# A second, tabulated order for the first work list of a three-stage kernel that plans its own instruction order

## The chip, the cores and the metric

The kernel runs on one core of one Trainium2 chip. The metric is the device time of one execution in microseconds (us); the median over the runs of a kernel is quoted. The core has five engines with instruction streams of their own: TensorE (PE; its weight loads are shown apart as PEld), VectorE (DVE), ScalarE (ACT), GpSimd (POOL) and SyncE (SP), which issues nearly all DMAs here. An instruction waits on semaphores for what it needs, and on one engine the instructions run in the order in which the program wrote them.

## The reference, cut to what matters

Three stages follow one another; the second takes the output of the first, the third that of the second.

```python
def attn(q, k, v):                  # 2 batches x 8 heads, 768 positions, 64 wide
    scores = q @ k.T / 8            # kept: window of 128 positions, and the first 4 (sinks)
    a = exp(scores - max); a /= sum(a) + 1e-09
    return a @ v                    # -> x, 2 x 768 x 512

def moe(x, w_gate, wq, wk, wv, wo): # 4 experts, every one over all tokens, causal
    logits = x @ w_gate; top 2 per token, w = softmax over the two
    for e in range(4):
        a = softmax(causal(x@wq[e] @ (x@wk[e]).T / 8))
        out += w[:, e] * (a @ (x@wv[e])) @ wo[e]

def moe2(x, w_gate, w_local, w1, w2):   # 8 experts of 512 x 1024 x 512, one per token
    fresh = argmax(x @ w_gate); p = softmax(x @ w_gate)
    e[s] = fresh[s] if s == 0 or sigmoid(x[s] @ w_local) < 0.5 else e[s-1]
    out[s] = p[s, e[s]] * relu(x[s] @ w1[e[s]]) @ w2[e[s]]
```

## The kernel before, in words

**The work.** Queries go in tiles of 128. A unit of attention work is a handful of score matrices: TensorE multiplies kT by qT into a PSUM bank (L699), VectorE adds the mask and takes the row maximum in one custom instruction (L713; its `nm` row is the maximum), ScalarE exponentiates (L723), TensorE transposes the result (L827), ScalarE copies the transposed block to float16 as the high half (L830), VectorE subtracts to get the low half (L834), and TensorE multiplies both halves by v (L842 to L844). In the second stage most of these halves are made before the transposition instead, by ScalarE (L782) and GpSimd (L787), and v is multiplied at L798 to L800. kT and qT come from transposes (L424) that ScalarE copies out of PSUM (L430). v of the first batch is scaled and split by ScalarE (L649) and VectorE (L653), later ones by GpSimd (L660, L663, L669); L609 takes the maxima of v for that scale, L532 joins them into `amax`, and L536 moves that across partitions. The sinks of one batch are gathered into `vbd` by GpSimd (L633 to L636). The first stage's result is scaled by L962 and L966 (the sums behind it by L339), the second's by L1098. Weights are split into a high and a low part by ScalarE (L478, later L1511 and L1513) and GpSimd or VectorE (L480, L1521). L1005 makes the low half of the second stage's v, L1025 to L1038 are the gate of the four experts, some dozen VectorE instructions on 128x8 numbers. The routing of the third stage (`route`) is a chain of small instructions: VectorE makes `r_ms` (L1296 to L1306), TensorE turns it (L1323), VectorE scans (L1327, L1329), TensorE turns back (L1335), VectorE makes the one-hot rows (L1337), TensorE counts with them (L1345, L1346), and VectorE turns counts into slots (L1350 to L1361) and these into permutations (L1369; GpSimd L1371). After that the lists of tokens are made, GpSimd writes the expert numbers `eui` (L1920), and SyncE loads the weights of the third stage's units by these numbers.

**The order.** None of this is written in the order in which it runs. Each piece is a `Task` with an engine, a planned duration, its dependences, the buffers that it takes (`acq`) and gives back (`rel`) and a priority, added to an `Order` object. `Order.run` is a greedy planner: it keeps a planned clock for each engine, takes the piece that can start first (ties by priority), books its planned duration, and emits its instructions at once. Durations come from formulas such as `d_v` (VectorE) and `d_a` (ScalarE), and latencies between engines from `LAT`; nothing in them depends on what another engine does at the time. `order.run()` of the first list covers the first two stages, the routing and the lists, some 250 us of the run; later calls plan the units of the third stage.

**Spins.** While the buffer "warm" is held (up to about 30 us, and again from about 205 us on), the planner puts idle matmuls of 128x512 (`spin`, L410) into the gaps that it foresees on TensorE: `int(gap / 0.22 * fill)` of them where a gap is over 0.3 us, with `fill` 0.5 in the first stretch and 1.0 in the second. They write to a bank that nobody reads, and TensorE executes them like any other matmul, in order.

Of the kernel before, what the change touches and what calls it, by code (L numbers as in the profile page):

```python
# [63 lines left out]
WT = (0, 3)  # L64
PC = 4
PSZ = 32
QU = 2
QN = 4
CLD = 0.4


class Task:
    __slots__ = ("eng", "dur", "fn", "deps", "acq", "rel", "prio", "end", "name", "rows", "fills", "lat", "slack", "hold")

    def __init__(self, eng, dur, fn, deps, acq, rel, prio, rows=False):
        self.eng, self.dur, self.fn, self.prio, self.rows = eng, dur, fn, prio, rows
        self.deps = [d for d in deps if d is not None]
        self.acq, self.rel = list(acq), list(rel)
        self.end = None
        self.fills = False  # L80
        self.lat = None
        self.slack = 0.0
        self.hold = 0.0


class Order:
# [7 lines left out]
    def __init__(self, bufs, named):  # L94
# [6 lines left out]
        self.fill = FILL  # L101
        self.rows = False

    def add(self, eng, dur, fn, deps=(), acq=(), rel=(), prio=0, rows=False):
# [21 lines left out]
    def run(self):  # L126
        todo = sorted(self.tasks, key=lambda t: t.prio)
        while todo:
            best = {}
            for part in (todo[:400], todo[400:]):  # L130
                for t in part:
                    e = self.ready(t)
# [18 lines left out]
            if t.eng == "PE" and "warm" in self.held and gap > 0.3:  # L151
                for _ in range(int(gap / 0.22 * self.fill)):
                    self.spin()
            t.end = e + t.dur
            self.free[t.eng] = t.end
            if t.eng == "PE":
                self.rows = t.rows
            for tag, name in t.acq:
                ring = self.slots[tag]
                k = min((i for i, x in enumerate(ring) if x is not None), key=lambda i: ring[i])  # L160
                self.held[name] = (tag, k)
                self.named[name] = self.bufs[tag][k]
                ring[k] = None
            for name in t.rel:
                tag, k = self.held.pop(name)
                self.slots[tag][k] = t.end + (t.lat or self.LAT[t.eng])
            todo.remove(t)
            t.fn()
        self.tasks = []

    def state(self):
# [40 lines left out]
def fused_kernel(  # L212
# [96 lines left out]
    K = {}  # L309
# [1225 lines left out]
    def turnover():  # L1535
        blocks_.close()
        own = ctx.enter_context(tc.tile_pool(name="own", bufs=1, side="right", reuse_waits="tile"))
        for tag, n, tiles in (("xg", 1, [([128, DM], F32)]), ("hs", 2, [([128, 512], F32)]),
# [6 lines left out]
                        + [K["S1", b, i, u] for b in range(B) for i in range(NT) for u in range(UN1)]  # L1545
                        + [K.get(("skm", b, i)) for b in range(B) for i in range(NT)], prio=at2(B - 1, 0))
    last_sc = []

# [186 lines left out]
    for t in order.tasks[n_:]:  # L1735
        t.fills = t.eng in ("PE", "ACT", "DVE")
    order.run()
    front.close()
# [257 lines left out]
```

## Time and profile before

| | |
|---|---|
| time, median of 3 runs | 409.21 us (409.04 to 410.77) |
| the profiled execution's own time | 411.15 us |
| its span, from first to last instruction | 409.4 us |
| TensorE clock granted over it, mean | 0.998 |
| VectorE busy, with 1005 rows | 325.1 us |
| ScalarE busy, with 758 rows | 317.9 us |
| GpSimd busy, with 288 rows | 166.8 us |
| DMA, all queues | 58.75 MB in 101501 packets |

The span is 1.75 us shorter than the execution's own time, which also holds what lies around the instructions, and the profiled execution is 1.94 us above the median of the timed runs. "Busy" counts an instruction from its start to its end, so a matmul that has been issued and is still flowing through the array counts as busy too. A timeline row joins consecutive instructions of one line and shape (its xcount) and gives their start, the time they cover, and in brackets how long the engine stood idle before and which instruction released it. A tile's name in the trace has no buffer number.

### The profile page before, as it was taken

How to read it: one execution, taken by the hardware profiler on the slowest of the kernel's cores; microseconds unless marked ns; L12 is line 12 of the kernel's file. 1: busy time of each engine (PE TensorE's matmuls, PEld its weight loads, DVE VectorE, ACT ScalarE, POOL GpSimd, SP SyncE). 2: the span in 40 equal slices, each digit the busy share in tenths (PEclk: the TensorE clock that was granted, in tenths of full speed). 3: DMA queues.
4: the chain of work that ended last, by engine and by line, in shares of the span. 5: the costliest groups of instructions: out<-in, count | busy, mean ns of one | idle time of the engine just before them, and what ended most of it. 6: DMA issues, size and time to landing. Idle time of an engine off the chain costs nothing. (4 is left out here: it accounts for less than half of the span.)

```text
span 409.4 us, 10290 instructions
## 1 busy us (share of the span) xinstructions
PE 394.5 (96%) x3339; PEld 312.8 (76%) x3339; DVE 325.1 (79%) x1005; ACT 317.9 (78%) x758; POOL 166.8 (41%) x288
## 2 busy tenths in 40 slices
PE   8899999999999999999998999999999999999993
PEld 4569988969879877988876777746666888888883
DVE  2998599497889688779899899866576788899680
ACT  4799799669999789965698428867577898888770
POOL 7378985267976637710627015020101310110100
PEclk9999999999999999999999999999999999999999
DMA  7998298824987743820561112958879951110001
GB/s 152 187 209 194 67 175 141 160 72 79 183 153 141 130 95 66 143 61 20 201 214 53 38 67 85 344 201 313 303 236 391 388 195 40 51 53 27 33 22 57
DMA packets 101501, 58.75 MB, mean 143 GB/s; under 512 B 83903, under 2 KB 85439, under 8 KB 101440
## 3 DMA queue, kind: packets, MB, share of 16 engines
q1 hardware_dynamic: 99280, 51.21, 49.3%
q0 software_dynamic: 2160, 6.82, 4.8%
q8 instruction: 28, 0.46, 0.4%
q14 instruction: 33, 0.27, 0.2%
HBM read 82.39 MB, written 6.55 MB: 217 GB/s over the span
## 5 line engine op out<-in xcount | busy, mean ns | idle before, releaser
L723 ACT ACTIVATE P<-P,nm 128x260 f32<-128x260 f32 (+3 forms) x100 | 53.1, 535 | 12.0 <-DVE nm L713 11.6
L713 DVE CUSTOM_DVE_ANT_0 P<-bank,masks 128x260 f32<-128x260 f32 (+3 forms) x84 | 36.5, 463 | 8.1 <-PE bank L699 8.0
L787 POOL TENSOR_TENSOR raw<-PX,raw 128x512 f16<-128x512 f32 (+2 forms) x34 | 35.6, 1051 | 16.5 <-ACT raw L782 14.4
L834 DVE TENSOR_TENSOR pT<-bank,pT 128x512 f16<-128x512 f32 (+1 forms) x50 | 30.7, 630 | 8.4 <-ACT pT L830 8.3
L699 PE MATMUL bank<-kT,qT 64*128 64x260 f32 (+1 forms) x192 | 31.8, 405 | 2.3 <-POOL kT L597 1.1
L723 ACT ACTIVATE PX<-PX,nm 128x260 f32<-128x260 f32 (+4 forms) x60 | 30.6, 513 | 2.5 <-DVE nm L713 2.4
L1521 DVE TENSOR_TENSOR wo<-raw,wo 128x1024 fp32r<-128x1024 f32 x23 | 27.8, 1220 | 3.2 <-ACT wo L1513 2.6
L424 PE MATMUL bank<-ident,raw 128*128 128x128 f32 x168 | 28.3, 292 | 1.2 <-DVE r L339 0.4
L830 ACT ACTIVATE pT<-bank 128x512 f16<-128x512 f32 (+1 forms) x50 | 26.0, 551 | 3.9 <-PE bank L827 3.6
L324 PE MATMUL bank<-xT,wqk_h 128*128 128x256 f32 x96 | 28.5, 297 | 0.0
L325 PE MATMUL bank<-xT,wqk_h 128*128 128x256 f32 x96 | 26.7, 278 | 0.0
L326 PE MATMUL bank<-xT,wqk_l 128*128 128x256 f32 x96 | 26.7, 278 | 0.0
L699 PEld LDWEIGHTS bank<-kT,qT 64*128 64x128 f32 x192 | 19.1, 191 | 9.9 <-issue 2.1
L827 PE MATMUL bank<-ident,P 128*128 128x128 f32 x180 | 26.5, 277 | 0.2 <-DVE nm L713 0.2
L1521 DVE TENSOR_TENSOR w<-raw,w 128x1024 fp32r<-128x1024 f32 x19 | 22.9, 1222 | 4.5 <-ACT w L1513 4.4
L1513 ACT ACTIVATE wo<-raw 128x1024 fp32r<-128x1024 f32 x23 | 24.0, 1057 | 3.0 <-PE bank L326 2.7
L424 PEld LDWEIGHTS bank<-ident,raw 128*128 128x128 f32 x168 | 20.5, 164 | 7.4 <-DVE nm L713 2.0
L713 DVE CUSTOM_DVE_ANT_0 PX<-bank,masks 128x260 f32<-128x260 f32 (+4 forms) x60 | 23.4, 426 | 2.4 <-PE bank L699 2.3
L699 PE MATMUL bank<-k,q 64*128 64x256 f32 (+3 forms) x128 | 24.4, 466 | 0.1
L1617 ACT ACTIVATE hs<-bank 128x512 f32<-128x512 f32 x24 | 14.4, 599 | 10.7 <-PE bank L326 10.7
L1521 DVE TENSOR_TENSOR wqk_l<-raw,wqk_h 128x1024 fp32r<-128x1024 f32 x17 | 20.8, 1226 | 2.3 <-ACT wqk_h L1513 2.2
L1689 POOL DMA_INDIRECT out_dram<-masks,six x6 | 6.9, 1147 | 38.2 <-ACT masks L1682 33.0
(504 smaller groups left out, 1467.9 us busy)
## 6 DMA issues: line engine op xcount, KB each, us to landing
raw<-in_moe_w_dram SPq DMA_DIRECT2D x96, 512.0 KB
qw<-in_moe_w_dram SPq DMA_DIRECT2D x32, 512.0 KB
raw<-in_v_dram SPq DMA_DIRECT2D x12, 256.0 KB
x2d<-x SPq DMA_DIRECT2D x12, 256.0 KB
raw<-in_q_dram SPq DMA_DIRECT2D x11, 256.0 KB
raw<-in_k_dram SPq DMA_DIRECT2D x11, 256.0 KB
pT<-raw SPq DMA_TRANSPOSE x46
raw<-in_moe_wv_dram SPq DMA_DIRECT2D x1, 512.0 KB
```

What stands on the lines that cost most here:

```text
L324: nc.tensor.matmul(o, l[0], r[0], start=start, stop=False)
L325: nc.tensor.matmul(o, l[0], r[1], start=False, stop=False)
L326: nc.tensor.matmul(o, l[1], r[0], start=False, stop=stop)
L424: nc.tensor.transpose(p[:, j * 128:(j + 1) * 128], src(j), ident)
L699: nc.tensor.matmul(o, l, r, start=True, stop=True)
L713: nc.vector.tensor_tensor_reduce(p, s, sg["mask"], 0.0 if dead and st == 1 else -scale, gr["nm"] if si else 3.0e38, op0=OP.add, op1=OP.min ...
L723: nc.scalar.activation(p, p, AF.Exp, bias=gr["nm"], scale=-1.0, accum_out=sg["sum"]())
L787: nc.gpsimd.tensor_sub(shaped(pl[:, s_], dims), p_, shaped(ph[:, s_], dims))
L827: nc.tensor.transpose(R[tk][:, j * 128:(j + 1) * 128], R[gr["P"]][:, c:c + 128], ident)
L830: nc.scalar.activation(R[sk_][:, :n * 128], R[tk][:, :n * 128], AF.Copy)
L834: nc.vector.tensor_sub(pl[:, :n * 128], R[tk][:, :n * 128], ph[:, :n * 128])
L1521: eng.tensor_sub(wl[:, :, s_], R["raw", u, c, hf][:, :, s_], f32(wh)[:, :, s_])
```

## The change

The greedy planner still runs over the first list, but while it runs it emits nothing: it assigns the buffers, notes for each piece what it took and gave, and collects the pieces in a list (`seq`). Then `flush` goes through a table of numbers, `TURNS`, and emits the collected pieces in that order. The list is cut in two at the piece `turnover` (`stays = True`), where the space of the first stage's blocks goes to buffers of the third stage; the table's first string has 1432 numbers for what comes before it, the second 407 for what comes after. Buffers, dependences, instructions and their sizes stay as they were. Only the number of spins is worked out anew, from the planned gaps of the new order by the same formula, with turn-round times `IN` and `OUT`. The table was computed beforehand; by the words that came with the change, with a plan that counts GpSimd's hold on VectorE's operations. Later lists are planned as before.

```diff
+IN, OUT = 0.095, 0.19
...
+TURNS = (
+    "0 2-16 19 21 17 24 20 22 18 23 28 25-27 29 1 30-32 37 33-36 38 41-43 48 40 55 47 39 45-46 50 52-53 44 49 54 "
...
+    "1-5 0 6 10 7 17 8 11 22 13 12 9 15 19 14 26 18 16 20 24-25 32 21 23 36 27 29 28 30-31 37 39 43 33 35 40-42 34 "
...
+def unpacked(texts):
+    runs = [[[int(x) for x in r.split("-")] for r in t.split()] for t in texts]
+    return [[n for r in rs for n in range(r[0], r[-1] + 1)] for rs in runs]
...
@@ Order.run @@
             if t.eng == "PE" and "warm" in self.held and gap > 0.3:
-                for _ in range(int(gap / 0.22 * self.fill)):
-                    self.spin()
+                if self.seq is None:
+                    for _ in range(int(gap / 0.22 * self.fill)):
+                        self.spin()
...
+                t.spins = self.fill if "warm" in self.held else False
...
-            t.fn()
+            if self.seq is None or t.stays:
+                self.flush()
+                self.go(t)
+                t.fn()
...
+            else:
+                self.seq.append(t)
...
+    def flush(self):
...
+        turns = self.turns.pop(0)
...
+        for n in turns:
+            t = seq[n]
...
+            if t.eng == "PE":
+                if t.spins and self.hot and gap > 0.3:
+                    for _ in range(int(gap / 0.22 * t.spins)):
+                        self.spin()
...
+            end[t] = free[t.eng] = e + t.dur
...
+            if t.eng != "J":
+                t.fn()
...
+    K["turnover"].stays = True
...
+    order.seq, order.turns = [], unpacked(TURNS)
     order.run()
```

Comparing the instruction streams of the two kernels: TensorE's real work stands in the same order, and 11 of the 37 spins are gone, six in the first stretch and five in the second; a few others stand elsewhere. SyncE's 823 rows, all the DMA issues on its queue among them, are the same in the same order. VectorE has the same 1089 rows (read accumulators counted apart), of which about 323 stand elsewhere, ScalarE the same 719 with about 151 elsewhere, GpSimd the same 343 with about 43 elsewhere. Behind the first list nothing differs. The lines of the change lie 139 or so below those of before: L713 is L852 there, L834 is L973, L609 is L748, L653 is L792, L339 is L478, L430 is L569, L478 is L617, L723 is L862, L830 is L969, L1306 is L1445, L1361 is L1500, L1369 is L1508, L1562 is L1702.

**First place: VectorE at about 14 to 17 us,** the first blocks of queries. P4 and P0 are masked scores, v0 and v1 the split v, vmax the maxima of the next v, r1 the reciprocal sums. Before:

```order
L653 SCALAR_TENSOR_TENSOR v0_1_100<-raw2_0_85,s_se0_461,v0_0_99 128x512
L609 TENSOR_REDUCE vmax0_236<-raw3_0_86 128x1
L653 SCALAR_TENSOR_TENSOR v1_1_102<-raw2_0_85,s_se0_461,v1_0_101 128x512
L339 TENSOR_REDUCE r1_0_0_237<-sums1_149 128x8
L609 TENSOR_REDUCE vmax0_236<-raw3_0_86 128x1
L962 RECIPROCAL r1_0_0_237<-r1_0_0_237 128x8
L713 ISA P4_0_111,nm_522<-bank7_82,masks_158 128x260
L713 ISA nm_522 128x1
L713 ISA P4_0_111,nm_525<-bank1_76,masks_158 128x260
```

And in the change:

```order
L792 SCALAR_TENSOR_TENSOR v0_1_100<-raw2_0_85,s_se0_469,v0_0_99 128x512
L748 TENSOR_REDUCE vmax0_236<-raw3_0_86 128x1
L852 ISA P4_0_111,nm_504<-bank7_82,masks_158 128x260
L852 ISA nm_504 128x1
L852 ISA P0_0_107,nm_506<-bank5_80,masks_158 128x260
L852 ISA nm_506 128x1
L852 ISA P4_0_111,nm_508<-bank1_76,masks_158 128x260
L852 ISA nm_508 128x1
L478 TENSOR_REDUCE r1_0_0_237<-sums1_149 128x8
```

The masks of P4 and P0 now stand right behind the first vmax. The second split of v (v1) has gone 19 rows down, behind the low half of pT0, and the second vmax stands behind four masks.

**Second place: ScalarE at about 25 to 31 us.** wvg_h and wqk_h are the high parts of the second stage's weights, kT the transposed keys of the third block. Before:

```order
L478 ACTIVATE wvg_h_208<-raw0_0_83 128x256 x4
L830 ACTIVATE pT2_0_114<-bank2_77 128x512
L830 ACTIVATE pT3_0_115<-bank4_79 128x512
L723 ACTIVATE P3_0_110,sums1_149<-P3_0_110,nm_650 128x260
L723 ACTIVATE P3_0_110,sums1_149<-P3_0_110,nm_657 128x260
L478 ACTIVATE wqk_h_206<-raw1_0_84 128x256 x4
L430 ACTIVATE kT_212<-bank3_78 128x4x128
```

And in the change:

```order
L969 ACTIVATE pT2_0_114<-bank2_77 128x512
L617 ACTIVATE wvg_h_208<-raw0_0_83 128x256
L969 ACTIVATE pT3_0_115<-bank4_79 128x512
L862 ACTIVATE P4_0_111,sums1_149<-P4_0_111,nm_668 128x260
L862 ACTIVATE P3_0_110,sums1_149<-P3_0_110,nm_647 128x260
L569 ACTIVATE kT_212<-bank3_78 128x4x128
L617 ACTIVATE wqk_h_206<-raw1_0_84 128x256
L617 ACTIVATE wvg_h_208<-raw0_0_83 128x256
L862 ACTIVATE P4_0_111,sums1_149<-P4_0_111,nm_671 128x260
```

Of the eight weight pieces that stood ahead of kT, seven stand behind it, spread singly over the next rows; one exponential of P4 has come ahead of it.

**Third place: VectorE at about 219 to 223 us,** the last tiles, where r_ms opens the last pass of the routing chain; slot and v2h belong to an earlier pass, ux is the input of a third-stage unit. Before:

```order
L834 TENSOR_TENSOR pT1_0_113<-bank2_77,pT1_0_113 128x512
L1358 TENSOR_SCALAR rk_319<-rk_319 128x2
L1304 TENSOR_REDUCE mxs_321<-LG_233 128x1
L1296 SCALAR_TENSOR_TENSOR r_fr10_334<-LG_233,s0_291 128x1
L1361 TENSOR_SCALAR slot_320<-rk_319 128x2
L1305 SCALAR_TENSOR_TENSOR r_sc10_332<-LG_233,mxs_321,rev8_286 128x8
L1369 TENSOR_SCALAR v2h0_215<-iot_287,slot_320,tok_294 128x128 x2
L1306 ISA r_sc10_332,r_ms10_333<-r_sc10_332,r_fr10_334 128x8
L1306 ISA r_ms10_333 128x1
L834 TENSOR_TENSOR pT3_0_115<-bank5_80,pT3_0_115 128x512
L1562 TENSOR_TENSOR ux0_1_3422<-bank4_79,ux0_0_3421 128x512
```

And in the change:

```order
L1435 SCALAR_TENSOR_TENSOR r_fr10_334<-LG_233,s0_291 128x1
L1444 SCALAR_TENSOR_TENSOR r_sc10_332<-LG_233,mxs_321,rev8_286 128x8
L1496 TENSOR_REDUCE rk_319<-r_sc8_330 128x2
L1702 TENSOR_TENSOR ux0_1_3416<-bank4_79,ux0_0_3415 128x512
L1445 ISA r_sc10_332,r_ms10_333<-r_sc10_332,r_fr10_334 128x8
L1445 ISA r_ms10_333 128x1
L1497 TENSOR_SCALAR rk_319<-rk_319 128x2
L973 TENSOR_TENSOR pT3_0_115<-bank5_80,pT3_0_115 128x512
L1500 TENSOR_SCALAR slot_320<-rk_319 128x2
L1466 TENSOR_SCALAR raw7_0_90<-bank2_77 1x128
L1508 TENSOR_SCALAR v2h0_215<-iot_287,slot_320,tok_294 128x128
```

The pieces of the earlier pass (rk, slot, v2h) that stood ahead of r_ms stand behind it, and the 128x512 piece of ux has come ahead of it.

## Rows read from the trace of the kernel before

**Rows 1.** The page's first part: busy time, share of the span and instructions.

```profile
PE 394.5 (96%) x3339; PEld 312.8 (76%) x3339; DVE 325.1 (79%) x1005; ACT 317.9 (78%) x758; POOL 166.8 (41%) x288
```

**Rows 2.** Busy time by stretch: length; PE, PEld, DVE, ACT, POOL; clock; DMA share; GB/s.

```profile
0.00:215.00 215.00, 208.87 (x2260) 173.60 (x2260) 173.35 (x754) 179.57 (x571) 129.59 (x241) 1.00 0.65 135
215.00:226.00 11.00, 9.89 (x115) 7.28 (x114) 10.93 (x44) 9.20 (x21) 7.89 (x18) 1.00 0.13 49
...
272.00:397.00 125.00, 125.00 (x645) 93.94 (x638) 98.05 (x96) 98.67 (x125) 16.20 (x16) 1.00 0.50 177
...
14.00:22.00 8.00, 7.31 (x74) 5.22 (x75) 8.00 (x25) 5.85 (x18) 0.00 (x0) 1.00 0.90 148
26.00:31.00 5.00, 4.67 (x48) 2.86 (x48) 4.86 (x22) 5.00 (x17) 4.70 (x7) 1.00 1.12 213
```

**Rows 3.** PE's waits, 0 to 215 us: line, releaser, total us, times, longest.

```profile
PE bank L699 <- POOL kT L597: 1.1, 1, 1.1
PE bank L699 <- DVE nm L713: 0.7, 1, 0.7
PE bank L424 <- DVE r L339: 0.4, 1, 0.4
```

**Rows 4.** Timeline at the first list's end, then the chain that ended last (start, us).

```profile
246.03 0.30 POOL L1920 CAST eui<-euf 36x3 int32<-36x3 f32 x1 [7.09 <-DVE euf L1919]
...
256.21 8.45 DMA qw<-in_moe_w_dram
```

**Rows 5.** The spins: their line over the run (ns min/median/max), and the first four.

```profile
L410 PE MATMUL bank<-v2h x37: 377/379/634, 1.3 to 243.6; 128*128 128x512 f16 x37
...
1.25 1.89 PE L410 MATMUL bank<-v2h 128*128 128x512 f16 x4 [1.25 <-DVE v2h L414]
```

**Rows 6.** Timeline, 14 to 18 us: DVE and PE (start, us, engine, line).

```profile
15.05 0.74 DVE L653 SCALAR_TENSOR_TENSOR v<-raw,s_se,v 128x512 f16<-128x512 f32 x1
15.79 0.67 DVE L609 TENSOR_REDUCE vmax<-raw 128x1 f32<-128x512 f32 x1
16.49 0.38 DVE L713 CUSTOM_DVE_ANT_0 P<-bank,masks 128x260 f32<-128x260 f32 x1
16.93 0.44 PE L827 MATMUL bank<-ident,P 128*128 128x128 f32 x2 [0.16 <-DVE nm L713]
17.21 0.59 PE L410 MATMUL bank<-v2h 128*128 128x512 f16 x2
```

**Rows 7.** Timeline, 28 to 36 us: ACT, POOL and PE.

```profile
28.84 1.33 ACT L478 ACTIVATE wqk_h<-raw 128x256 fp32r<-128x256 f32 x4
30.07 0.59 ACT L430 ACTIVATE kT<-bank 128x512 f32<-128x512 f32 x1
30.51 2.79 POOL L480 TENSOR_TENSOR wvg_l<-raw,wvg_h 128x256 fp32r<-128x256 f32 x4
35.82 0.39 PE L324 MATMUL bank<-wvg_h,xT 128*128 128x260 f32 x1
```

**Rows 8.** DVE beside GpSimd: L1036 over the run (ns min/median/max); timeline at 84 and 132 us.

```profile
L1036 DVE TENSOR_SCALAR g_mx<-g_mx x6: 163/170/1135, 44.4 to 193.7; 128x2 f32<-128x2 f32 x6
...
84.43 1.50 DVE L653 SCALAR_TENSOR_TENSOR v<-raw,s_sv,v 128x512 f16<-128x512 f32 x1
132.56 3.56 POOL L787 TENSOR_TENSOR raw<-P,raw 128x512 f16<-128x512 f32 x4 [1.23 <-ACT raw L782]
132.61 1.14 DVE L1036 TENSOR_SCALAR g_mx<-g_mx 128x2 f32<-128x2 f32 x1
```

**Rows 9.** PE's weight loads: waits, 148 to 162 us.

```profile
PEld bank L699 <- DVE nm L713: 0.7, 2, 0.5
```

**Rows 10.** Timeline, 220 to 223 us: DVE and PE.

```profile
220.25 0.51 DVE L1361 TENSOR_SCALAR slot<-rk 128x2 int32<-128x2 int32 x1
221.09 0.98 DVE L1369 TENSOR_SCALAR v2h<-iot,slot,tok 128x128 f16<-128x128 f32 x2
222.49 0.27 PE L1323 MATMUL bank<-ident,r_ms 128*1 128x128 f32 x1 [0.81 <-DVE r_ms L1306]
```

More of the change, by code (lines that the diff above doesn't have):

```diff
@@ L69 @@
 CLD = 0.4
+TURNS = (
[63 rows of a table added]
+)
+def unpacked(texts):
+    runs = [[[int(x) for x in r.split("-")] for r in t.split()] for t in texts]
+    return [[n for r in rs for n in range(r[0], r[-1] + 1)] for rs in runs]
 class Task:
-    __slots__ = ("eng", "dur", "fn", "deps", "acq", "rel", "prio", "end", "name", "rows", "fills", "lat", "slack", "hold")
+    __slots__ = ("eng", "dur", "fn", "deps", "acq", "rel", "prio", "end", "name", "rows", "fills", "lat", "slack", "hold", "took", "gave", "spins", "stays")
     def __init__(self, eng, dur, fn, deps, acq, rel, prio, rows=False):
@@ L83, in __init__ @@
         self.hold = 0.0
+        self.took, self.gave, self.spins, self.stays = [], [], False, False
 class Order:
@@ L102, in __init__ @@
         self.rows = False
+        self.seq, self.turns, self.hot = None, [], None
+        self.then = {"DMA": 0.8}, {}, {}, [False]
     def add(self, eng, dur, fn, deps=(), acq=(), rel=(), prio=0, rows=False):
@@ L161, in run @@
                 self.held[name] = (tag, k)
-                self.named[name] = self.bufs[tag][k]
+                t.took.append((name, tag, k))
                 ring[k] = None
@@ L165, in run @@
                 tag, k = self.held.pop(name)
+                t.gave.append((tag, k))
                 self.slots[tag][k] = t.end + (t.lat or self.LAT[t.eng])
             todo.remove(t)
-            t.fn()
-        self.tasks = []
+            if self.seq is None or t.stays:
+                self.flush()
+                self.go(t)
+                t.fn()
+                self.then[1][t] = max(self.then[1].get(d, 0.0) for d in t.deps) if t.stays else 0.0
+            else:
+                self.seq.append(t)
+                if t.eng == "J":
+                    t.fn()
@@ new lines, in run, with go, wait @@
+        self.flush()
+        self.seq = None
+        self.tasks = []
+    def go(self, t):
+        for name, tag, k in t.took:
+            self.named[name] = self.bufs[tag][k]
+            if name == "warm":
+                self.hot = tag, k
+    def wait(self, d, t):
+        return self.SAME.get(t.eng, 0.0) if d.eng == t.eng else d.lat or self.LAT[d.eng]
+    def flush(self):
+        if not self.seq:
+            return
+        seq, self.seq = self.seq, []
+        free, end, slots, rows = self.then
+        ins, gave, held = set(seq), {}, {}
+        for t in seq:
+            held[t] = [gave[x[1:]] for x in t.took if x[1:] in gave]
+            gave.update((x, t) for x in t.gave)
+        turns = self.turns.pop(0)
+        assert sorted(turns) == list(range(len(seq)))
+        done = set()
+        for n in turns:
+            t = seq[n]
+            assert all(d in done or d not in ins for d in t.deps + held[t])
+            done.add(t)
+            e = free.get(t.eng, 0.0)
+            gap = -e
+            if t.eng == "PE" and t.rows != rows[0]:
+                e += IN if t.rows else OUT
+            for d in t.deps:
+                e = max(e, end.get(d, 0.0) + self.wait(d, t))
+            for _, tag, k in t.took:
+                e = max(e, slots.get((tag, k), 0.0))
+            gap += e
+            if t.eng == "PE":
+                if t.spins and self.hot and gap > 0.3:
+                    for _ in range(int(gap / 0.22 * t.spins)):
+                        self.spin()
+                rows[0] = t.rows
+            end[t] = free[t.eng] = e + t.dur
+            for x in t.gave:
+                slots[x] = end[t] + (t.lat or self.LAT[t.eng])
+                if x == self.hot:
+                    self.hot = None
+            self.go(t)
+            if t.eng != "J":
+                t.fn()
```

61 rows, old and new, of the table TURNS are left out of this document.

## Prediction

> **What bounds the kernel now.** I read the busy shares first: TensorE is busy for 96% of the span, VectorE and ScalarE for some 78% each, GpSimd for 41% [rows 1]. A change that leaves TensorE's real work alone can only win where TensorE stands or spins, so the second view is the busy time by stretch [rows 2]. In 272 to 397 us TensorE has no gap (125.00 of 125.00), and the change does not reach there. In 0 to 215 us it stands for 215.00 − 208.87 = 6.1 us, in 215 to 226 for 11.00 − 9.89 = 1.1 us. Spins count as busy: they last 377 ns each, but a row of two lasts 0.59, so each further one adds 0.22 us [rows 5, 6]. The 37 of them hold some 8 us, most of them lying before 31 us or after 205. Thus about 15 us lie open in the first list, of which the start (the first wait of 1.25 and the first four spins, [rows 5]) is not touched.
>
> Third, the waits: the named ones of 0 to 215 us are few, 1.1 for kT, 0.7 and 0.4 for VectorE the largest [rows 3], and in 215 to 226 us, 0.81 for r_ms [rows 10]. VectorE is full where they fall: 8.00 of 8.00 in 14 to 22 us, 10.93 of 11.00 in 215 to 226 [rows 2]. There its order decides which matmul waits.
>
> Fourth, what makes VectorE's pieces long: L1036 takes 170 ns as a rule and 1135 once, at 132.61, while GpSimd works through four pieces of L787; L653 takes 0.74 at 15.05, where GpSimd is idle, and 1.50 at 84.43 beside GpSimd's work [rows 2, 6, 8]. Added up over the rows that exceed their usual duration beside GpSimd, the holds come to some 10 us over 28 pieces: my estimate, of which these rows are the largest cases. The old planner books none of it.
>
> Last, what a gain is worth. The lists end in `eui` at 246.03 us; SyncE then issues loads whose longest takes 8.45 us from 256.21 and stands in the chain that ended last [rows 4]. The work that leads to `eui` follows TensorE's last tiles, so I pass what TensorE gains before 226 us through whole.
>
> **The change, part by part** (a gain is positive; bounds in brackets). TensorE's order and SyncE's are unchanged, so no matmul is moved and no DMA issue passes another; loads move only with the buffers that they wait for.
>
> *Start, to 14.3 us: −0.3 [−0.7 to +0.4].* TensorE waits 1.1 us for kT [rows 3], behind ScalarE's first split of v, behind amax and its scale. In the new order one mask that needs a later matmul stands ahead of the second vmax, so amax comes later. A mask takes 0.38, a vmax 0.67 [rows 6]; I take a mask less some overlap. The best case is a mask gained.
>
> *14 to 22 us: +0.2 [−0.9 to +0.8].* The masks of P4 stood behind v1, r1, a vmax and a reciprocal, and L827 waited for the bank: 0.16 at 16.93, with one spin ahead and two behind it [rows 6]. 0.16 + 3 × 0.22 = 0.8 goes. But four new spins, 0.9 us, stand around L536 some four us later, since the vmax pieces have been put back. VectorE is full here and loses one L653 (0.74) ahead of pT0, so part of that is covered. I take little.
>
> *26 to 31 us: +1.1 [0 to +1.4].* kT is copied at 30.07, behind four weight pieces of 1.33 [rows 7] and four more before those. Seven of eight now stand behind it: 7 × 0.33 = 2.3, less one exponential put ahead, at most as long as kT's own 0.59. TensorE's open time here is 5.00 − 4.67 = 0.33 of standing [rows 2] and nine spins, 2.0 us; four spins stay (0.9), so at most 1.4 can go. What covers the late weight pieces: GpSimd's half of them ends at 30.51 + 2.79 = 33.30 and TensorE first asks at 35.82 [rows 7], 2.5 us of slack, of which the spreading uses perhaps 2; if more, the gain here is eaten, hence the lower bound of 0.
>
> *88 us: +0.3 [0 to +0.7].* The wait of 0.7 for nm [rows 3] comes after the held L653, 0.76 longer than unheld [rows 6, 8]; that piece now stands eight rows earlier, and the scale chain and routing sums behind it move with it.
>
> *137 us: +0.3 [0 to +0.4].* The gate pieces L1032 to L1038, the held L1036 among them [rows 8], leave the row ahead of L1098; the wait of 0.4 is the cap [rows 3].
>
> *148 to 162 and 204 to 212 us: +0.6 [0 to +1.1].* Weight loads wait 0.7 us for nm in the 14 us of the first stretch [rows 9]; at that rate the 22 us of both hold 1.1, an estimate. I take about half, since matmuls in flight hide part of a late weight load.
>
> *215 to 226 us: +1.3 [0 to +2.2].* L1361 (0.51), two L1369 (0.98) and smaller pieces stood ahead of r_ms and now stand behind it, while L1562, a 128x512 piece like the vmax of 0.67 [rows 6], has come ahead: 1.49 − 0.67 = 0.8 net, and TensorE's wait for r_ms is 0.81 [rows 10]. Five of the eight late spins go. TensorE's open time here is 1.1 of standing and six spins, 1.3 us, less one spin that stays: 2.2 at most. I take the wait and half a microsecond of the routing chain behind it.
>
> The sum is −0.3 + 0.2 + 1.1 + 0.3 + 0.3 + 0.6 + 1.3 = **3.5 us**, with the bounds −1.6 to 7.0. The profiled execution took 411.15, so its like would take 407.6; the median of the runs is 409.21, 1.94 lower, and I forecast 409.21 − 3.5 = **405.7 us**. About 0.5%, 2.05 us, is what a measurement of this kernel can tell from no change: faster is below 407.16, slower above 411.26.
>
> **The rivals.**
>
> *The hold only moves.* VectorE and GpSimd do the same work in the same 226 us, and VectorE is full at the places that count [rows 2]. If the held pieces meet other GpSimd pieces, the terms from 88 us on are lost and −0.3 + 0.2 + 1.1 = 1.0 is left: 408.2. For it: 241 GpSimd rows keep it busy for 129.59 of 215 us, so a piece moved by a few rows easily meets another. Against it: the waits named have single large holds ahead of them [rows 8]. The Trainium skill, page "SBUF — State Buffer", section "Who interferes with whom", bears on this: the port pair that the two engines share is locked for a whole instruction by whichever starts first, and the other one stands still. By that rule a plan that puts VectorE's piece first would make GpSimd wait instead, and nothing is lost only as long as nobody needs GpSimd's result; the trace agrees as far as L1036's 1.14 beside L787 goes.
>
> *Everything gives.* All terms at their upper bounds, 7.0 us: 402.2. For it: the named waits of [rows 3] are few, so each that goes is not followed by another at once. Against it: it needs the start too.
>
> *The spins were needed (slower).* Eleven of 37 are gone. The clock is granted at 1.00, the 2.4 GHz level, in all these stretches [rows 2], yet the first spins take up to 634 ns against 377 [rows 5], 1.68 times as long, so TensorE can run slower than at the full rate at least at the start. If a thinner 215 to 226 us ran at that rate, its 9.89 us of work [rows 2] would take 6.7 us more: 405.7 + 6.7 = 412.4. It decides from 8.2 us of such work on, where the price passes 3.5 + 2.05. Against it: the stretch stays over 85% busy without the spins. The Trainium skill, page "TensorE: Matmul & The Clock Gate", section "What's actually happening", names the lower of the two levels, 1.2 GHz, for an engine that has been idle; by it the price would be 9.9 us, an estimate.
>
> *It acts off the path.* What goes had covered other waits, for instance a DMA or ScalarE's exponentials, and TensorE stands elsewhere as long: 409.2.
>
> **How the numbers follow.** The forecast case has 0.57 (its own range 404.0 to 407.1, each large term one step up or down), the moved hold 0.17, no effect 0.08, everything 0.10, the needed spins 0.08. Faster: 0.57 + 0.10 = 0.67. Same: 0.17 + 0.08 = 0.25. Slower: 0.08. The range goes from 402.2, the case in which everything gives, past the moved hold to 409.0; outside it lie the needed spins, the case without effect and the edge of the lowest, 0.2 in all.
>
> **What would show it.** Right: in the new trace kT's copy ends some 1.5 us earlier against the matmuls around it, and the L699 behind it waits less than 0.1; the wait of L1323 for r_ms is under 0.2; no L1036 or L653 takes over twice its usual time; TensorE stands for about 5 us in 0 to 215 and under 0.6 in the stretch that was 215 to 226; `eui` comes at about 242.5. Wrong: `eui` earlier by 3 us and the end not (the loads or the lists would then bound); a sum of waits as before with other names (the hold moved); matmuls of one shape longer or a granted clock under 1.00 in the first list (the spins); a new wait of TensorE for wvg_l at about 34 us or for amax at about 20.

## The result, and the profile after

The change takes **412.15 us**, the median of 22 runs (410.11 to 415.29), against 410.46 us for the kernel before in 22 runs (408.88 to 411.86): the ratio is 1.0052, 95% interval 1.0036 to 1.0067. So it is slower, by 1.7 us where 3.5 us less were forecast, and outside the range. One caution ahead of the traces: the profiled execution of the change took 410.11 us, the shortest of its 22, that of before 411.15, above its median. Laid side by side, the two would make the change look faster.

Busy shares and stretches of the change, answering to [rows 1, 2]. First the page's first part:

```profile
PE 391.2 (96%) x3328; PEld 310.2 (76%) x3328; DVE 326.0 (80%) x1005; ACT 318.2 (78%) x758; POOL 169.2 (41%) x288
```

Then busy time by stretch, columns as in [rows 2]:

```profile
0.00:215.00 215.00, 205.46 (x2219) 169.80 (x2220) 173.43 (x749) 177.81 (x564) 129.46 (x240) 1.00 0.66 135
215.00:226.00 11.00, 10.55 (x123) 8.10 (x122) 10.84 (x42) 9.67 (x26) 5.39 (x13) 1.00 0.07 27
...
40.00:60.00 20.00, 17.40 (x182) 15.60 (x182) 15.70 (x60) 15.87 (x53) 16.00 (x27) 1.00 0.49 98
```

In 215 to 226 us TensorE stands for 0.45 us instead of 1.1, as forecast. In 0 to 215 it stands for 215.00 − 205.46 = 9.5 instead of 6.1, and 2.6 us of that lie in 40 to 60 us (0.6 before), where the prediction had no term. The named waits of TensorE from 0 to 226 us say where (columns of [rows 3]):

```profile
PE bank L463 <- DVE v2l L1144: 1.6, 1, 1.6
...
PE bank L838 <- ACT P L862: 1.1, 1, 1.1
...
PE bank L1075 <- DVE g_mx L1176: 0.6, 1, 0.6
```

The waits for the reciprocal `r` (0.4) [rows 3] and for r_ms (0.81) [rows 10] are gone. The matmul of the start that waited 1.1 us for kT [rows 3] still waits 1.1, now for ScalarE's P (L862). The largest, 1.6 us for `v2l`, is new. The timeline of the change around it (columns of [rows 6]):

```profile
38.97 0.71 ACT L617 ACTIVATE wqk_h<-raw 128x256 fp32r<-128x256 f32 x2
...
40.07 0.41 ACT L617 ACTIVATE wqk_h<-raw 128x256 fp32r<-128x256 f32 x1
40.38 0.46 ACT L1140 ACTIVATE v2h<-bank,s_sw 128x256 f16<-128x256 f32 x1
...
41.59 0.47 ACT L1140 ACTIVATE v2h<-bank,s_sw 128x256 f16<-128x256 f32 x1
41.95 0.17 ACT L1141 ACTIVATE lg<-bank 128x4 f32<-128x4 f32 x1
...
40.56 2.80 POOL L619 TENSOR_TENSOR wqk_l<-raw,wqk_h 128x256 fp32r<-128x256 f32 x4
...
42.15 0.16 DVE L1164 TENSOR_REDUCE g_mx<-lg 128x2 f32<-128x8 f32 x1 [3.73 <-ACT lg L1141]
42.23 0.49 DVE L1167 TENSOR_TENSOR g_eq<-lg 128x32 f32<-128x32 f32 x1
42.75 0.29 DVE L1082 TENSOR_TENSOR skT<-bank,skT 32x128 f16<-32x128 f32 x1
43.05 0.35 DVE L1168 TENSOR_TENSOR g_gt<-lg 128x32 f32<-128x32 f32 x1
43.44 0.88 DVE L1144 SCALAR_TENSOR_TENSOR v2l<-bank,s_sw,v2h 128x256 f16<-128x256 f32 x2
...
44.07 0.36 PE L463 MATMUL bank<-xT,wqk_h 128*128 128x256 f32 x1 [1.62 <-DVE v2l L1144]
```

And the same pieces in the kernel before:

```profile
37.98 0.49 ACT L1001 ACTIVATE v2h<-bank,s_sw 128x256 f16<-128x256 f32 x1
39.38 0.50 ACT L1001 ACTIVATE v2h<-bank,s_sw 128x256 f16<-128x256 f32 x1
40.23 1.34 ACT L478 ACTIVATE wqk_h<-raw 128x256 fp32r<-128x256 f32 x4 [0.15 <-DMA raw<-in_moe_wk_dram]
...
38.57 0.48 DVE L1005 SCALAR_TENSOR_TENSOR v2l<-bank,s_sw,v2h 128x256 f16<-128x256 f32 x1 [0.62 <-ACT lg L1002]
39.98 0.48 DVE L1005 SCALAR_TENSOR_TENSOR v2l<-bank,s_sw,v2h 128x256 f16<-128x256 f32 x1 [0.74 <-ACT lg L1002]
40.81 0.16 DVE L1025 TENSOR_REDUCE g_mx<-lg 128x2 f32<-128x8 f32 x1
```

Before, ScalarE made `v2h` twice and then four weight pieces in a row, and VectorE made each `v2l` as its `v2h` came, ahead of the gate. In the change these four weight pieces, the high parts of wk, stand ahead of and between the two `v2h`, the last of which comes 2.2 us later. They are not the pieces that had been put behind kT at 26 to 31 us; the last two of those are done by 34.93:

```profile
34.20 0.73 ACT L617 ACTIVATE wqk_h<-raw 128x256 fp32r<-128x256 f32 x2
```

VectorE's row has the first gate piece next, which needs the last `lg`, so VectorE stands idle for 3.73 us with one `v2h` ready since 40.84; then four pieces of gate and sinks (beside GpSimd's `wqk_l`, L1167 takes 0.49 and L1168 0.35; L1167 takes 0.18 in another run below) run ahead of `v2l`. In the kernel's text `v2l` is the piece that gives back the PSUM bank of v, and it is `v2l` that TensorE's next matmul waits for.

**The whole list, by offsets.** TensorE's real matmuls stand in the same order in all kernels, so the start of each can be compared. The reference trace is that of the first experiment, the planner's own order run through the change's new code: its time is that of the kernel before. The table gives by how many us a matmul comes later (+) than in that trace (worked out, a median over the matmuls within 0.45 us):

| at, us | 15 | 26 | 31 | 41 | 44 | 50 | 71 | 85 | 88 | 103 | 135 | 138 | 144 | 160 | 204 | 212 | 226 |
|---|---|---|---|---|---|---|---|---|---|---|---|---|---|---|---|---|---|
| the change | −0.34 | −0.21 | −1.12 | −1.11 | +0.99 | +1.85 | +1.74 | +2.48 | +1.61 | +2.60 | +2.98 | +2.44 | +3.18 | +2.71 | +3.35 | +3.14 | +1.75 |
| only the middle (e4) | −0.07 | −0.09 | −0.09 | −0.09 | +1.81 | +2.67 | +2.57 | +3.30 | +2.44 | +3.41 | +3.58 | +3.04 | +3.69 | +3.23 | +4.02 | +4.03 | +4.04 |
| only the ends (e13) | −0.57 | −0.44 | −1.35 | −0.59 | −0.59 | −0.59 | −0.60 | −0.63 | −0.60 | −0.59 | −0.66 | −0.66 | −0.66 | −1.00 | −0.41 | −0.61 | −2.01 |

The change is 1.1 us ahead at 41 us, loses 3.0 us by 50, loses and wins until 204, and wins 1.4 us in 212 to 226. The 3.0 us are three steps: 0.3 at 42 us, 1.8 at the matmul that waits for `v2l`, 0.9 at the one that waits for `g_mx`. Single traces have a spread of their own: the five others whose order up to 31 us is the planner's lie between −0.4 and +0.6 at 15 us.

### The profile page after: what moved, and what is told of

It is laid out like the page before. It is cut to its first block, busy times and chain, and to the rows that moved or that the text cites. A ratio compares the mean times of both kernels' runs of the same rounds, so it can differ in the third digit from the quotient of the medians.

```text
span 408.4 us, 10242 instructions
## 1 busy us (share of the span) xinstructions
PE 391.2 (96%) x3328; PEld 310.2 (76%) x3328; DVE 326.0 (80%) x1005; ACT 318.2 (78%) x758; POOL 169.2 (41%) x288
## 4 chain that ended last, share of the span: by engine, by line
PE 48%; DVE 5%; issue 3%; DMA 1%; POOL 1%; ACT 0%; POOLq 0%; DVEq 0%
PE bank L463 12%; PE bank L465 11%; PE bank L464 11%; PE bank L1964 4%; PE bank L1695 4%; DVE P L852 2%; PE bank L838 2%; DMA pT<-raw 1%; PE bank L966 1%; PE bank L1295 1%; DVE pT L973 1%; POOL raw L926 1%; PE bank L563 0%; PE bank L983 0%; PE bank L981 0%
## 5 line engine op out<-in xcount | busy, mean ns | idle before, releaser
L862 ACT ACTIVATE P<-P,nm 128x260 f32<-128x260 f32 (+4 forms) x100 | 53.2, 535 | 6.7 <-DVE nm L852 6.7
L852 DVE CUSTOM_DVE_ANT_0 P<-bank,masks 128x260 f32<-128x260 f32 (+3 forms) x84 | 37.3, 464 | 8.3 <-PE bank L838 8.1
L973 DVE TENSOR_TENSOR pT<-bank,pT 128x512 f16<-128x512 f32 (+1 forms) x50 | 31.0, 630 | 6.6 <-ACT pT L969 6.2
L862 ACT ACTIVATE PX<-PX,nm 128x260 f32<-128x260 f32 (+4 forms) x60 | 30.7, 515 | 2.0 <-DVE nm L852 1.9
L969 ACT ACTIVATE pT<-bank 128x512 f16<-128x512 f32 (+1 forms) x50 | 26.5, 552 | 4.7 <-PE bank L966 3.7
L852 DVE CUSTOM_DVE_ANT_0 PX<-bank,masks 128x260 f32<-128x260 f32 (+4 forms) x60 | 23.7, 427 | 1.8 <-PE bank L838 1.8
L838 PEld LDWEIGHTS bank<-kT,qT 64*128 64x128 f32 x192 | 18.2, 185 | 8.7 <-issue 2.3
L1715 POOL DMA_INDIRECT xg<-x2d,gix x7 | 7.1, 1010 | 37.9 <-PE bank L1695 34.7
```

What stands on the lines that cost most here:

```text
L838: nc.tensor.matmul(o, l, r, start=True, stop=True)
L852: nc.vector.tensor_tensor_reduce(p, s, sg["mask"], 0.0 if dead and st == 1 else -scale, gr["nm"] if si else 3.0e38, op0=OP.add, op1=OP.min ...
L862: nc.scalar.activation(p, p, AF.Exp, bias=gr["nm"], scale=-1.0, accum_out=sg["sum"]())
L969: nc.scalar.activation(R[sk_][:, :n * 128], R[tk][:, :n * 128], AF.Copy)
L973: nc.vector.tensor_sub(pl[:, :n * 128], R[tk][:, :n * 128], ph[:, :n * 128])
```

## The experiments

Numbers in the table stand for pieces in the planner's sequence. Pieces 0 to 214 are what the planner puts before about 31 us, 215 to 399 lie at 31 to 51 us, and the second string is what lies behind the turnover. Most experiments keep the change's code and use the table's order inside some spans only, the planner's elsewhere (`SPANS` stands for the numbers that each run has in its place):

```diff
+def window_(turns, spans):
+    out, at = [], 0
+    for lo, hi in spans:
+        out += list(range(at, lo)) + [n for n in turns if lo <= n < hi]
+        at = hi
+    return out + list(range(at, len(turns)))
...
-    order.seq, order.turns = [], unpacked(TURNS)
+    order.seq, order.turns = [], [window_(t, s) for t, s in zip(unpacked(TURNS), SPANS)]
```

**The machinery and the spins.** `SPANS = ((), ())` is the planner's order (35 spins).

> The change's machinery with the planner's own order in both parts of the list: every engine's real work as in the kernel before, 35 spins instead of 37. Theory W (waits: pieces moved between 31 and 205 us make TensorE wait anew) and theory C (clock: the eleven missing spins let the granted clock fall in a part of the executions) both expect the time of the kernel before, 409.5 to 411.5 us. Its mean granted clocks, run by run, are the base for the others: C expects 0.995 or more in nearly all of them.

Measured: 410.27 us against 410.44, ratio 0.999 (0.9974 to 1.0005). Emitting from a list costs nothing that shows, so the loss lies in the order or in the spins.

```diff
+                t.idle = int(gap / 0.22 * self.fill)
...
-                if t.spins and self.hot and gap > 0.3:
-                    for _ in range(int(gap / 0.22 * t.spins)):
+                if t.spins and self.hot:
+                    for _ in range(t.idle):
```

> The change's order with the 37 spins of the kernel before, each ahead of the same matmul as there. C: mean granted clocks of 0.996 or more in all runs and about 410.5 to 411 us, the time that the change takes in its runs at such clocks. W: clocks spread as with the change (0.983 to 0.999), median 412 or a little over, since the spins only fill time in which TensorE waits.

Measured, the table's order with the 37 old spins: 413.63 us, 1.0076 (1.0048 to 1.0104). The missing spins are not the cause; the rival falls.

**The ends against the middle.** `SPANS = (((0, 215),), ((0, 407),))`, and its complement, `(((215, 1432),), ())`.

> The table's order only for the first 215 pieces (to about 31 us) and for the part behind the turnover (from about 185 us), the planner's order between; 26 spins. W: the gains of the two ends stay (about 2 us by 31 us, about 2 us from 205 to 226) and the losses between go: 406 to 408. C: the same 26 spins, so clocks spread as with the change and a median of 410 to 412.

> The table's order only for the pieces from the 215th to the turnover (about 31 to 185 us), the planner's order at both ends; 35 spins. W: all of the loss and none of the gain: 413 to 415. C: clocks of 0.996 or more, and about the time of the kernel before, 410 to 411.

Measured: the ends 408.45 us, 0.9948 (0.9931 to 0.9965); the middle 413.76 us, 1.0073 (1.0048 to 1.0099). The order between 31 us and the turnover costs some 3 us, and the rest of the table gains 2.

**Which part of the middle.** The change without pieces 215 to 399, and these pieces alone.

> The table's order for all pieces but the 215th to the 399th (about 31 to 51 us), which stand in the planner's order; 26 spins. W: the 2.7 us that TensorE loses between 31 and 49 us go, what is lost from 100 us on stays: 409 to 410.3, clocks of 0.994 or more. C in its first form (26 spins) would keep clocks under 0.99 in a third of the runs.

> The table's order only for the 215th to the 399th piece, the planner's elsewhere; 35 spins. W: most of the loss of the middle (3.3 us) is here: 412.4 to 413.4. If the middle's loss is spread over 31 to 205 us instead: under 411.5.

Measured: without them 409.41 us, 0.9964 (0.995 to 0.9978); these alone 411.98 us, 1.0032 (1.0019 to 1.0045). These 185 of 1432 pieces make the difference between a gain and a loss. They do it alone, with kT and the eight weight pieces of 26 to 31 us where the planner has them: ScalarE makes wk's pieces first, VectorE waits for the last `lg`, and the same matmul waits, here for ScalarE's `x`, which ends with the first `v2l` (at 45.09 and some 45.07). The timeline of pieces 215 to 399 alone:

```profile
40.11 0.72 ACT L626 ACTIVATE wqk_h<-raw 128x256 fp32r<-128x256 f32 x2 [0.20 <-DMA raw<-in_moe_wk_dram]
...
43.31 0.16 DVE L1173 TENSOR_REDUCE g_mx<-lg 128x2 f32<-128x8 f32 x1 [4.14 <-ACT lg L1150]
...
45.22 0.36 PE L472 MATMUL bank<-xT,wqk_h 128*128 128x256 f32 x1 [1.02 <-ACT x L648]
```

From 41 to 50 us its matmuls lose 2.4 us (offsets +0.57 and +3.00), those of the middle alone 2.8. So this loss is not the price of the early kT.

**One pair of pieces.** The two L1144 (pieces 274 and 285) put ahead of the gate pieces L1164, L1167, L1082 and L1168; nothing else is moved.

```diff
+    t_ = order.turns[0]
+    for n in (274, 285):
+        t_.remove(n)
+    t_[t_.index(291):t_.index(291)] = [285, 274]
```

> The change with one edit on VectorE: the two pieces of L1144 (low half of the second stage's v, from PSUM) stand ahead of the gate's first four pieces (L1164, L1167, L1082, L1168) instead of behind them. Theory W: TensorE's wait of 1.62 us for v2l at about 42 us falls under 0.4, the time by 1.0 to 1.4 us against the change, to 410.7 to 411.4. If the standstill of TensorE is also what lets the clock fall in some executions, no run is under 0.993 in clock and the median comes lower, 410.0 to 410.7. If the wait is really ScalarE's lateness, the wait stays over 1 us.

Measured: 409.83 us, 0.9986 (0.997 to 1.0002), against the change's 1.0052: 2.7 us for two rows on one engine. Each `v2l` now runs as its `v2h` comes, the gate behind them, and TensorE's matmul waits 0.56 (timeline of this kernel):

```profile
40.76 0.48 DVE L1144 SCALAR_TENSOR_TENSOR v2l<-bank,s_sw,v2h 128x256 f16<-128x256 f32 x1 [2.51 <-ACT lg L1141]
41.98 0.48 DVE L1144 SCALAR_TENSOR_TENSOR v2l<-bank,s_sw,v2h 128x256 f16<-128x256 f32 x1 [0.74 <-ACT lg L1141]
42.38 0.15 DVE L1164 TENSOR_REDUCE g_mx<-lg 128x2 f32<-128x8 f32 x1
42.45 0.18 DVE L1167 TENSOR_TENSOR g_eq<-lg 128x32 f32<-128x32 f32 x1
...
42.52 0.38 PE L463 MATMUL bank<-xT,wqk_h 128*128 128x256 f32 x1 [0.56 <-DVE v2l L1144]
```

TensorE waits 1.1 us less there, and its wait for `g_mx` behind it is gone too: from 41 to 50 us its matmuls lose 0.8 us against the reference trace, where those of the change lose 3.0. The median fell by 2.7. To see where the rest lies, the change was run again, beside new runs of the kernel before, and the same pair was put later instead, behind L1170.

> The change itself, beside the next three on the same chip. Both theories expect 411.5 to 413 again. If the clock falls in some executions because TensorE stands for 1.6 us at about 42 us, two to four of some ten runs have a mean granted clock under 0.992, and they are the longest.

> The change with the two pieces of L1144 put four gate pieces further back still (behind L1170). W, as a dose: TensorE's wait at about 42 us grows from 1.6 to 2.4 to 2.8 us and the time by about 1 us against the change. If the wait also lets the clock fall, more than half of the runs have a mean granted clock under 0.992, the median rises by 2 us or more, and the trace shows a stretch at the lower clock right behind the wait. If the clock has another cause, the share of such runs stays at about a third.

Measured: the change 410.99 us against 409.08, 1.0052 (1.0028 to 1.0077) once more; the pair put later 413.92 us, 1.013 (1.0086 to 1.0173), with a wait of 3.75. The second profile of the change caught what the first had not. Its stretches and its timeline:

```profile
44.00:45.00 1.00, 0.00 (x0) 0.02 (x1) 0.97 (x3) 0.59 (x2) 1.00 (x3) 1.00 0.00 0
45.10:48.40 3.30, 3.30 (x17) 3.30 (x17) 1.06 (x6) 0.69 (x3) 3.22 (x7) 0.50 0.02 5
48.50:52.00 3.50, 3.50 (x33) 3.50 (x32) 2.33 (x9) 1.73 (x6) 2.10 (x4) 1.00 0.33 75
```

```profile
45.01 0.52 PE L463 MATMUL bank<-xT,wqk_h 128*128 128x256 f32 x1 [1.91 <-DVE v2l L1144]
45.33 0.41 PE L464 MATMUL bank<-xT,wqk_h 128*128 128x256 f32 x1
45.55 0.41 PE L465 MATMUL bank<-xT,wqk_l 128*128 128x256 f32 x1
```

The first trace of the change has the same matmuls, behind the wait of 1.62, at the full clock:

```profile
44.26 0.28 PE L464 MATMUL bank<-xT,wqk_h 128*128 128x256 f32 x1
44.38 0.28 PE L465 MATMUL bank<-xT,wqk_l 128*128 128x256 f32 x1
```

TensorE had stood for 1.91 us; then the granted clock is 0.50, the 1.2 GHz level, from about 45 to 48.5 us. In that stretch the matmuls start 0.21 us apart instead of 0.12. It happens in some executions only: 7 of the change's 22 runs show a mean clock of 0.983 to 0.990 and have a median of 414.96 us; the other 15, at 0.994 or more, 411.53. In the second set 4 of 12, at 0.982 to 0.992, have 413.25 and the other 8 have 410.07. So the order by itself costs some 1.0 us in either set (411.53 against 410.46, 410.07 against 409.08), and the runs at the lower clocks, some 3.3 us longer and a third of all, move the median by another 0.6 to 0.9. One fall explains less than that: from 44 to 47 us the second trace loses 1.6 us against the first, and 3.4 us at 0.50 take 0.004 off the mean clock of a run of 410 us. Runs at 0.983 must hold more such stretches (an estimate from these numbers), and no trace caught one, so where they lie is open. With the pair ahead of the gate (wait 0.56) none of 12 runs is below 0.994, with the pair later (3.75) four of six are; but the trace of the latter has 0.994 and a stretch at 0.50, from 46.0 to 49.4, so a mean of 0.994 does not exclude one, and the 1.0 us may hold some of it. With the middle alone (wait 1.18) and with pieces 215 to 399 alone (1.02) none of 13 are below 0.995.

**The last part alone.** `SPANS = ((), ((0, 407),))`.

> The table's order only behind the turnover (from about 185 us on), the planner's before it; 31 spins. By the traces of the earlier runs the first 215 pieces gain 1.2 us by 30 us and have given 1.0 of it back by 44.6 us, and the last part gains 1.6 by 226 us. So this alone should keep nearly all that the two ends gave together: 408.4 to 409.2. If instead the early gain counted to the end, it would come out at 409.3 or more.

Measured: 409.48 us, 0.9985 (0.9964 to 1.0006): a gain that this run can't tell from none.

**Building the best version.** Two more edits, ScalarE's `v2h` pieces (272 and 282) ahead of the weight pieces as well, and then this with the table only where the offsets had fallen, pieces 0 to 399, 600 to 769 (about 88 us), 1010 to 1084 (about 137 us), and behind the turnover.

> The change with L1144 ahead of the gate pieces and, on ScalarE, the two pieces that make the high half (L1140) ahead of five weight pieces (L617) and two exponentials. W: the wait that was left at about 42 us (0.6 in the run with L1144 alone) is gone too; 408.8 to 409.8, clocks of 0.994 or more.

> The two edits of the last, and the table's order kept only where the traces show a gain: pieces up to 400 (to about 51 us), 600 to 769 (76 to 99 us), 1010 to 1084 (130 to 138 us) and behind the turnover; the planner's order elsewhere. By the offsets: 1.2 by 31 us, 0.3 at 87, 0.5 at 136 and 1.5 at 226 us: 3 us or more under the kernel before, 406.5 to 407.5. If waits merely change places, 408.5 or more.

Measured: 409.78 us, 1.0026 (1.0007 to 1.0046), and 409.50 us, 1.0008 (0.999 to 1.0026). Neither beats the kernel before; the 409.78 lies within the times expected, but beside a kernel before that takes 409.08 here, 1.4 us less than in the first result. In the second one's trace TensorE waits 0.41 at 43.89 and never that long otherwise between 15 and 52 us, yet the clock falls all the same, right behind 16 matmuls of 9 columns. These alone do not do it: the reference trace has the same 16 in 1.85 us at 44.55, and the clock stays at 1.00 there. The timeline and the stretch:

```profile
43.89 0.38 PE L481 MATMUL bank<-xT,wqk_l 128*128 128x256 f32 x1 [0.41 <-POOL wqk_l L635]
...
45.50 1.91 PE L660 MATMUL bank<-wg,x 128*128 128x9 f32 x16
47.27 0.43 PE L479 MATMUL bank<-xT,wqk_h 128*128 128x256 f32 x1
```

```profile
47.50:50.80 3.30, 3.30 (x17) 3.30 (x17) 1.91 (x8) 0.59 (x2) 3.30 (x7) 0.50 0.33 75
```

Thirteen of the 24 runs of these two kernels have a mean clock of 0.987 to 0.992.

So the ends were run again, beside new runs of the kernel before, and with them two more: the ends with the two middle places but not the stretch of 31 to 51 us, and the ends with that stretch but not the two places.

> The kernel of the third run once more (table ahead of piece 215 and behind the turnover, the planner's order between). Theory A (the gain of the two ends is real and the middle loses it): 0.995 of the kernel before, within 0.993 to 0.9965. Theory B (the third run's 0.995 belonged to its chip): 0.999 to 1.002, as the combination of the twelfth run gave.

> The ends and the two places in the middle where the offsets fell, pieces 600 to 769 (about 88 us) and 1010 to 1084 (about 137 us), without pieces 215 to 399. Theory A (these places gain by themselves): 1 to 1.5 us shorter than the ends alone, 0.991 to 0.993. Theory B (each piece of the table's order pays back at its seams what it gains): as the ends alone or up to 1 us longer, 0.995 to 0.998.

> The ends and pieces 215 to 399 with both v2 edits (the low halves ahead of the gate pieces, the high halves ahead of the weight pieces), the planner's order elsewhere. Theory A (with the edits the stretch of 31 to 51 us costs nothing more): as the ends alone, 0.994 to 0.996. Theory B (this stretch still loses, and it is what took the gain of the twelfth run): 1 to 2 us longer than the ends alone, 0.998 to 1.001, and the granted clock falls to 0.5 in its trace at 43 to 50 us.

Measured: 406.86 us against 408.65, **0.9948** (0.9927 to 0.9969); 407.18 us, 0.995 (0.9933 to 0.9968); 409.25 us, 1.0004 (0.9988 to 1.002). The gain of the ends is real; the two places add nothing; the stretch of 31 to 51 us takes the whole gain even with both edits, though the fall of the clock that was expected is not in its trace. That trace, at full clock, shows two losses: GpSimd starts on the low parts of wk at 41.55 us (at 39.60 in the version of the ends), and TensorE's weight loads wait for these (first line, from the waits of 40 to 62 us); and a matmul waits for the DMA that brings its pT.

```profile
PEld bank L481 <- POOL wqk_l L635: 0.6, 2, 0.4
...
59.81 0.20 PE L953 MATMUL bank<-v,pT 128*128 128x64 f16 x1 [0.86 <-DMA pT<-raw]
```

Against the ends its matmuls are 0.4 us ahead at 41 us, 0.7 behind at 44, 1.7 behind at 60 (worked out as above).

**How the ends' gain is made up.** The first part alone, `(((0, 215),), ())`, beside the last part alone again.

> The table ahead of piece 215 alone, the planner's order from there on and behind the turnover. Theory A (the two ends add up): about 1 us shorter than the kernel before, 0.996 to 0.9985, and with the next run's gain the 2 us of the two ends together. Theory B (what the start gains up to 31 us is given back by 44 us, as the traces' offsets fall from 1.4 to 0.6 us between 31 and 35): 0.9985 to 1.0005, and the ends' gain is nearly all from behind the turnover.

> The table behind the turnover alone, once more. Theory A (the ends add up): about 1 us shorter than the kernel before, 0.997 to 0.9985, as in the fifth run. Theory B (the ends' gain is nearly all from here): 0.995 to 0.997.

Measured: 410.07 us against 410.08, 1.0002 (0.9987 to 1.0018), and 409.03 us, 0.9977 (0.9963 to 0.9991). The first part gains nothing that reaches the end, the last part 1.0 us. That both together gave 0.9948 twice is more than the sum, 0.9979; the intervals overlap (0.9927 to 0.9969 for the ends, 0.9963 to 0.9991 for the last part), so whether there is more than the sum stays open.

The version that beats both kernels is thus the one of the ends, 0.9948 of the kernel before twice, each time beside other runs of that kernel (12 and 7 runs).

## Why the prediction was wrong, step by step

The step that failed is the sum's silence on 31 to 205 us: the prediction counted the named waits there that would go, and gave no term to the pieces that the table puts back there. The offsets lose 6.4 us there, 3.0 of them at 41 to 50 us, where wk's four weight pieces go ahead of `v2h` and the gate goes ahead of `v2l`; which pieces cost the other 3.4 was not tried one by one. By the offsets of the change:

| step | forecast gain | gain in the offsets |
|---|---|---|
| start to 14.3 us | −0.3 | +0.3, with the clock's start in it |
| 14 to 22 us | +0.2 | −0.1 |
| 26 to 31 us | +1.1 | +0.9 |
| 88 us | +0.3 | +0.9 |
| 137 us | +0.3 | +0.5 |
| 148 to 162, 204 to 212 us | +0.6 | +0.5 and +0.2 |
| 215 to 226 us | +1.3 | +1.4 |
| sum of these | +3.5 | +4.6 |
| 41 to 50 us | none | −3.0 |
| 71 to 85 us | none | −0.7 |
| 88 to 103, 103 to 135 us | none | −1.0, −0.4 |
| 138 to 144, 160 to 204 us | none | −0.7, −0.6 |

Together, 4.6 − 6.4 = −1.8, the offset at 226 us (50 to 71 us gives 0.1 back). The +0.3 of the start tells nothing, since traces of one order differ by more there. `eui` shows that the offset passes through whole up to there, as the prediction had it: it comes 1.79 us later than in the reference trace, and 1.90 earlier in the version of the ends. The lines of three kernels, the reference trace, the change and the ends, each from its timeline:

```profile
245.08 0.30 POOL L2066 CAST eui<-euf 36x3 int32<-36x3 f32 x1 [7.09 <-DVE euf L2065]
```

```profile
246.87 0.30 POOL L2061 CAST eui<-euf 36x3 int32<-36x3 f32 x1 [6.33 <-DVE euf L2060]
```

```profile
243.18 0.29 POOL L2066 CAST eui<-euf 36x3 int32<-36x3 f32 x1 [6.41 <-DVE euf L2065]
```

Behind `eui` a single trace shows it no longer (last section). That −1.8 is so near to the 1.7 of the medians is thus in part luck: this trace has no fall of the clock, and the runs without a low mean clock lose some 1.0.

**26 to 31 us: right, and kept up to 41 us.** kT is copied early and its matmuls wait for nothing:

```profile
27.71 0.58 ACT L569 ACTIVATE kT<-bank 128x512 f32<-128x512 f32 x1
...
28.40 0.71 PE L838 MATMUL bank<-kT,qT 64*128 64x260 f32 x4
```

The prediction checked the cover of the late weight pieces against `wvg_l` at 34 us and found 2.5 us of slack; the offsets bear it out, −1.12 at 31 us and −1.11 at 41. What is lost behind 41 us has another source: the experiments on pieces 215 to 399 lose it with kT at its old place. The gain needs the table's order behind it, though. When only the first part is moved, the offset goes from −1.05 at 31 us to −0.58 at 35 and −0.30 at 41, and no gain is left at the end.

**88 and 137 us: the cap was too low, and the pieces landed.** Each place gained more than its named wait. Yet the version with these places and the ends is no faster than that with the ends, so what they gain is paid back around them: its offset is −0.54 at 71 us and −0.50 at 103, −0.48 at 135 and −0.30 at 144. Which piece pays was not tried one by one.

**215 to 226 us: right.** 1.4 us in the offsets, 1.0 in the time by the run of the last part alone.

**The rivals.** *The hold only moves* was right on the hold and too kind on the price. Added up over the rows that exceed their usual duration beside GpSimd before 226 us, holds come to some 9 to 10 us in the kernel before, in the change and in the version of the ends alike (estimates; they depend on what is called usual). New places in the change, from its timeline:

```profile
47.81 0.98 DVE L1173 SCALAR_TENSOR_TENSOR gate<-g_rk,gate 128x8 f32<-128x8 f32 x1
48.83 0.16 DVE L1174 TENSOR_REDUCE g_mx<-gate 128x2 f32<-128x8 f32 x1
49.03 1.17 DVE L1175 TENSOR_SCALAR g_mx<-g_mx 128x2 f32<-128x2 f32 x1
```

The 1.17 at 49.03 is the L1036 of [rows 8], now where TensorE waits 0.6 for `g_mx`; at 132.61, where it was held before, the largest wait that followed was the 0.4 for `r` [rows 3]. The version of the ends keeps the old hold and is the fastest:

```profile
130.87 1.14 DVE L1180 TENSOR_SCALAR g_mx<-g_mx 128x2 f32<-128x2 f32 x1
```

What a hold costs is thus not its length but what is behind it. The Trainium skill, page "SBUF — State Buffer", section "Who interferes with whom", says that a reduction never contends with GpSimd, while a piece with two inputs in SBUF or a two-port `tensor_scalar` does; the rows at 47.81 to 49.03 agree, with 0.16 for the reduction between 0.98 and 1.17. *The spins were needed* had the right sign and the wrong cause, and that its 412.4 is so near to the 412.15 is luck: bringing them back gave 1.0076, and the clock fell at 45 us, far from any spin, behind a wait that the new order made. *It acts off the path* and *everything gives* are excluded by the result as they were priced, though most of the terms came, and 88 and 137 us went as the former says.

## What to carry to other kernels

When a table moves many pieces, follow each piece that goes back to the next matmul that needs it, through every engine's row on the way, and not just to its own reader; a static row turns one late input into a stop for all that is behind it. Try a new order by stretches: here two stretches held a gain of 0.5% that 185 pieces between them turned into a loss. And look at the mean clock of every run, since a wait may cost more in some executions than the one trace shows.

## What the runs showed of the hardware that was not expected

A standstill of TensorE of 1.9 us in the middle of a run was followed by 3.3 us or more at granted clock 0.50 in the trace, and the kernels with such a wait (1.6 to 1.9) show a mean clock of 0.992 or less in 14 of 44 runs (7 of 22, 4 of 12, and 3 of 10 with the old spins); those with waits of 1.0 to 1.2 us in none of 13. This one wait is not the whole of it: the two kernels with 0.4 us there have 0.992 or less in 13 of 24. The Trainium skill, page "TensorE: Matmul & The Clock Gate", section "What's actually happening", names 1.2 GHz for an engine that has been idle; the trace agrees with 0.50 at 45.10 to 48.40. That a run can lose the clock with no wait over 0.41 us between 15 us and the fall at 47.4, as the combined version's did, was seen in one trace and not explained. A second wait comes and goes between executions: TensorE is busy for 19.28 us of 252 to 272 in the reference trace and for all 20.00 in the change's, where no `qw` transfer holds it up.

```profile
252.00:272.00 20.00, 19.28 (x100) 12.18 (x98) 17.86 (x19) 16.27 (x21) 5.46 (x5) 1.00 0.70 243
```

```profile
252.00:272.00 20.00, 20.00 (x121) 13.53 (x119) 19.36 (x23) 18.18 (x25) 6.77 (x5) 1.00 0.67 239
```

By the offsets the change's trace comes 1.80 us late at 258 us and 0.38 at 272. Over all traces the offset moves by −2.0 to +0.8 there, and by −1.8 and +0.5 in the two traces of the one version of the ends. So where a single trace ends says little of its order; the medians do.
